# Reordering the prologue, the column sums and the kept outputs of a chunked linear-attention and MLP kernel

## The chip, the cores and the metric

The kernel runs on one core of a Trainium2 chip. A core has five engines that run their own instruction queues in order and meet at semaphores: TensorE (PE in the profile; its weight loads are listed as PEld), VectorE (DVE), ScalarE (ACT), GpSimd (POOL) and SyncE (SP). DMAs are issued here by SP's queue (SPq) and, for a few, by ScalarE's (ACTq). The metric is device time in microseconds of one execution. The kernel before takes 203.81 us, the median of three runs (203.07 to 204.19).

## The reference

Inputs are q, k, v and alpha, each (4 batches, 8 heads, 768 positions, 48), and the weights w_in (384 x 2048), w_out (2048 x 384) and two scalars s and b, all float32.

```python
# per batch and head, for t = 0..767
state = alpha[t][:, None] * state + outer(k[t], v[t])
y[t]  = q[t] @ state
# then, with x = y of all heads side by side, (3072, 384)
h   = x @ w_in
g   = s * relu(h)**2 + b
out = g @ w_out
```

## The kernel before

**Blocks.** The 3072 rows are 24 blocks of 128 positions, six per batch. Within a block the recurrence is written as matrix products; from block to block of a batch a state is carried. All of a block's work is cut into steps, each a small function that issues instructions on one or more engines. `n` or `g` is the block, `u` a quarter.

- `ln(n)` (ScalarE, L200): logarithm of alpha. `cum(n)`: running sums by a matmul with a triangular matrix (L207), then ScalarE's two exponentials `bi_sb` (L218) and `b_sb` (L219). For block 0 to 4 the block's decay comes from further small matmuls; for later blocks `decay(n)` takes it through DRAM by three small DMAs on SP (L227, L229).
- `qk(n)` (VectorE): `kb = k * bi` (L235) and `qb = q * b` (L236). `vcast(n)` (GpSimd, L203): v to bf16.
- `tr(n)`: eight transposes on TensorE (L241), and VectorE's copy of them, `qkT` (L246). `amat(n)`: eight matmuls (L256) that give the scores, and VectorE's two multiplications with the mask, `am_a` and `am_b` (L264).
- `yp(n)`: the block's y from the carried state (L275) and the masked scores (L284), the state's update (L295), and ScalarE's copy of y to bf16 (L302). `st(n)`: the state (VectorE L329 or L331, GpSimd L336 and L340). `xt(n)`: three transposes of y (L309) and ScalarE's copy (L315).
- `mp`, `rl`, `sq` of a block and quarter: 12 matmuls with w_in (L362), ScalarE's relu (L376), VectorE's square (L383). `mr` is the first two, `m` all three.
- `o(n, u)`: 4 matmuls with w_out (L397) that accumulate in one PSUM bank over the four quarters; the last evicts. For the first `NKEEP = 5` blocks ScalarE copies the result into a buffer of its own, `keep_sb` (L406), and VectorE adds the bias later, `add_bias` (L417). For all others VectorE adds the bias while it evicts (L410). Then SP stores (L414).

The scalar s is folded into w_out when it is cast to bf16. The scalar b becomes a row that is added to every output row: b times the column sums of w_out. `colsum(1..7)` (VectorE, L172 and L174, 128 x 768 float32 each) add up eight parts of w_out, `bias_sum` (L177) halves the result once more, and `bias_row` (three times two float32 matmuls L181, and ScalarE's L182) sums over partitions.

**Weights.** w_in comes in four quarters and w_out in four, by DMA in float32. `win(i)` casts a quarter of w_in: one third by ScalarE (L151), two thirds by VectorE (L153). `wout(i)` casts a quarter of w_out: the even ones by ScalarE (L165), the odd ones by VectorE (L157).

**Order.** The order on every engine is written by hand. Each step is put into a list with a position, and the list is sorted by it. A block has 8 positions: block n's `yp` and `st` are at 8n, and its other steps at fixed distances before and after. In the later blocks `cum` is 14.8, `tr` 10.8 and `amat` 7.9 positions ahead of `yp`; for blocks 5 to 7 the distances grow from 7.0, 4.8 and 2.2 to these. The start, with blocks 0 to 3 and the preparation of block 4, is an explicit list (positions 0 to about 10). Where TensorE would have nothing to do there, `busy(n)` issues n matmuls whose result nobody reads (L190).

**Loads.** SP issues the loads of blocks 0 and 1, w_in, w_out and the blocks up to 7, in an order of their own; there are 8 buffers per input. `early(2)` issues alpha and k of block 2 from ScalarE's queue.

Of the kernel before, what the change touches and what calls it, by code (L numbers as in the profile page):

```python
# [8 lines left out]
FP32 = mybir.dt.float32  # L9
BF16 = mybir.dt.bfloat16  # L10
AF = mybir.ActivationFunctionType
# [3 lines left out]
def kernel(  # L15
# [12 lines left out]
    nc = tc.nc  # L28
# [6 lines left out]
    d_model = moe_w_in.shape[0]  # L35
    d_ff = moe_w_in.shape[1]
    NJ = d_ff // 128
    KT = d_model // 128
# [4 lines left out]
    NLD = 8  # L43
# [19 lines left out]
    def ring(name, shape, dtype, n):  # L63
        return [sb.tile(shape, dtype, name=f"{name}{i}") for i in range(n)]
# [25 lines left out]
    t1_sb = sb.tile([128, NP, 96], FP32, name="t1_sb")  # L90
    sc_sb = sb.tile([128, NP, 96], FP32, name="sc_sb")
    sd_sb = ring("sd_sb", [128, NP, 96], BF16, 2)
    r_sb = ring("r_sb", [128, 512], BF16, 6)
    out_sb = ring("out_sb", [128, d_model], FP32, 3)
    xd_all = sb.tile([128, UNITS, KT * C], BF16, name="xd_all")
    gt_all = sb.tile([128, UNITS, NJ * C], BF16, name="gt_all")
# [7 lines left out]
    w_in_st = sb.tile([128, KT, d_ff], FP32, name="w_in_st")  # L104
    w_in_bf = sb.tile([128, KT, d_ff], BF16, name="w_in_bf")
# [2 lines left out]
    cs_sb = sb.tile([128, 2, d_model], FP32, name="cs_sb")  # L108
    bias_w = sb.tile([128, d_model], FP32, name="bias_w")

    NKEEP = 5
    keep_sb = ring("keep_sb", [128, d_model], FP32, NKEEP)


    def src(t, n):
        b, c = n // NCH, n % NCH
        return t[b, :, c * C : (c + 1) * C, :].rearrange("h s d -> s h d")

    def load_a(n, eng=None):
        (eng or nc.sync).dma_start(out=al_sb[n % NLD], in_=src(alpha, n))  # L120

    def load_q(n, eng=None):
        (eng or nc.sync).dma_start(out=q_sb[n % NLD], in_=src(q, n))

    def load_k(n, eng=None):
        (eng or nc.sync).dma_start(out=k_sb[n % NLD], in_=src(k, n))

    def load_v(n, eng=None):
        (eng or nc.sync).dma_start(out=v_sb[n % NLD], in_=src(v, n))

    def load(n):
        if n < NBLK:
            load_a(n)
            load_k(n)
            load_q(n)
            load_v(n)

    def load_w_in(i):
        cols = slice(i * d_ff // 4, (i + 1) * d_ff // 4)
        nc.sync.dma_start(  # L140
            out=w_in_st[:, :, cols], in_=moe_w_in[:, cols].rearrange("(t r) f -> r t f", t=KT)
        )

    def load_w_out(j0, j1):
        nc.sync.dma_start(
            out=w_out_st[:, j0:j1],
            in_=moe_w_out[128 * j0 : 128 * j1, :].rearrange("(j r) m -> r j m", r=128),
        )

    def cast_w_in(c0, c1):  # L150
        nc.scalar.activation(out=w_in_bf[:, 0, c0:c1], in_=w_in_st[:, 0, c0:c1], func=AF.Copy)  # L151
        for kk in (1, 2):
            nc.vector.tensor_copy(out=w_in_bf[:, kk, c0:c1], in_=w_in_st[:, kk, c0:c1])  # L153

    def cast_w_out(j0, j1):
        if j0 // 4 % 2 == 1:
            nc.vector.tensor_scalar(  # L157
                out=w_out_bf[:, j0:j1],
                in0=w_out_st[:, j0:j1],
                scalar1=s_col,  # L160
                scalar2=None,
                op0=ALU.mult,
            )
        else:
            nc.scalar.activation(  # L165
                out=w_out_bf[:, j0:j1], in_=w_out_st[:, j0:j1], func=AF.Copy, scale=s_col
            )
# [177 lines left out]
    nrelu = [0]  # L345


    h_in_o = {(2, 2), (2, 3)}
    h_of = {}

    def mp(g, u):
# [39 lines left out]
    def mm2(g, t, u):  # L391
# [12 lines left out]
        if u == 3:  # L404
            if g < NKEEP:
                nc.scalar.activation(out=keep_sb[g], in_=op[:, 0:d_model], func=AF.Copy)  # L406
# [18 lines left out]
    quarter = d_ff // 4  # L425
# [3 lines left out]
    load_v(2)  # L429
    load_w_in(2)  # L430
    load_w_in(3)
    load(3)
    for j in range(0, NJ, 4):
        load_w_out(j, j + 4)
    for n in range(4, NLD):
        load(n)
    make_upper_triangular(nc, U_bf, 1.0, diag=True)
    for t in la_sb:
# [14 lines left out]
    def at(pos, fn, *args):  # L453
        events.append((pos, len(events), fn, args))
# [3 lines left out]
        st(n)  # L458

    def wout(i):  # L460
        cast_w_out(4 * i, 4 * i + 4)

    def early(n):
        load_a(n, nc.scalar)
        load_k(n, nc.scalar)

    def win(i):
        cast_w_in(i * quarter, (i + 1) * quarter)

    def m(g, u):  # L470
        mp(g, u)
# [11 lines left out]
    for pos, what in enumerate(  # L483
        [
            (ln, 0), (vcast, 0), (cum, 0), (qk, 0), (spread,), (busy, 3), (tr, 0), (busy, 1), (ln, 1), (vcast, 1), (amat, 0),
            (cum, 1), (early, 2), (busy, 3), (yp, 0), (qk, 1), (st, 0), (busy, 1), (tr, 1), (xt, 0), (busy, 2), (amat, 1),
            (win, 0), (win, 1), (busy, 5), (yp, 1), (mr, 0, 0), (st, 1), (busy, 1), (xt, 1), (mr, 0, 1), (ln, 2), (sq, 0, 0),
            (sq, 0, 1), (m, 1, 0), (cum, 2), (mr, 1, 1), (vcast, 2), (qk, 2), (sq, 1, 1), (busy, 4), (tr, 2), (busy, 3),
            (amat, 2), (busy, 5), (yp, 2), (win, 2), (st, 2), (busy, 2), (xt, 2), (m, 2, 0), (m, 2, 1), (ln, 3), (mr, 0, 2),
            (mr, 1, 2), (cum, 3), (vcast, 3), (win, 3), (sq, 0, 2), (sq, 1, 2), (qk, 3), (m, 2, 2), (mr, 0, 3), (mr, 1, 3),  # L490
            (tr, 3), (sq, 0, 3), (sq, 1, 3), (mr, 2, 3), (amat, 3), (sq, 2, 3), (wout, 0), (busy, 4), (yp, 3), (st, 3),
            (wout, 1), (o, 0, 0), (xt, 3), (o, 1, 0), (o, 2, 0), (m, 3, 0), (m, 3, 1), (wout, 2), (o, 0, 1), (o, 1, 1),
            (colsum, 1), (m, 3, 2), (ln, 4), (m, 3, 3), (wout, 3), (o, 2, 1), (cum, 4), (o, 0, 2), (vcast, 4), (qk, 4),
            (o, 1, 2), (o, 2, 2), (colsum, 2), (tr, 4), (o, 1, 3), (colsum, 3), (o, 2, 3), (amat, 4), (colsum, 4), (o, 0, 3),
        ]
    ):
        at(0.1 * pos, *what)


    for i, pos in ((5, 35.6), (6, 39.4), (7, 43.4)):  # L500
        at(pos, colsum, i)
    at(47.4, bias_sum)
    for i in range(3):
        at(51.2 + i, bias_row, i)
    for n in range(NKEEP):
        at(61.3 + 8 * n, add_bias, n)
        at(62.2 + 8 * n, store, n, keep_sb[n])
    for u in range(4):
        at((30.5, 31.5, 33.5, 36.5)[u], o, 3, u)
    at(20.0, load, NLD)  # L510
    for n in range(4, NBLK):
        p = 8 * n
        if n > 4:
            f = min((n - 5) / 3.0, 1.0)
            c, t, a = 7.0 + 7.8 * f, 4.8 + 6.0 * f, 2.2 + 5.7 * f
            at(p - c - 1.9, ln, n)
            at(p - c + 0.01, vcast, n)
            at(p - c, cum, n)
            at(p - c + 0.2, qk, n)
            at(p - t, tr, n)  # L520
            at(p - a, amat, n)
        at(p, y, n)
        if n + 5 < NBLK:
            at(p - 4.0, load, n + NLD - 3)
        for u in range(4):
            at(p + (2.5, 3.5, 5.5, 7.5)[u], m, n, u)
            at(p + (8.5, 9.5, 12.5, 14.5)[u], o, n, u)
        at(p + 1.0, xt, n)
# [32 lines left out]
```

## Time and profile before

| | |
|---|---|
| median of 3 runs | 203.81 us |
| the profiled execution | 203.28 us, of which the instructions span 201.4 us |
| TensorE busy | 184.3 us (92%), 2430 matmuls |
| VectorE busy | 153.6 us (76%) |
| ScalarE busy | 116.8 us (58%) |
| GpSimd busy | 58.6 us (29%) |
| granted TensorE clock | 1.0 throughout |
| DMA | 30.33 MB, mean 151 GB/s; 106611 of 113310 packets under 512 B |
| the 34 fill matmuls (L190) | 10.2 us of TensorE's busy time |
| chain that ended last | TensorE 71%, ScalarE 4%, VectorE 3% |

A row of a timeline gives the start, the duration, engine, line, operation, the tile written and those read, the shape and the count; in brackets stands how long the engine was idle just before, and what ended that. Matmuls are pipelined: one of 128 columns lasts 0.22 us in its row, but they follow each other every 0.056 us, so a chain of them is read by its length and not by its sum. The chain view follows the end of the run back, at each step to what released it.

### The profile page before, as it was taken

What the parts mean: (1) busy time and instruction counts of PE and PEld (TensorE: products, weight loads), DVE (VectorE), ACT (ScalarE), POOL (GpSimd) and SP (SyncE); (2) the same over time, 40 slices, a digit from 0 to 9 for tenths busy, and PEclk for the clock granted to TensorE, in tenths of its full rate; (3) what the DMA queues carried; (4) which work ended last, traced back from release to release, by engine and by line L of the source; (5) the groups of instructions that cost most, each with busy time, mean ns of one, the idle gap of its engine ahead of it and who ended that gap; (6) DMA issues with size and microseconds to landing.
All of it is one profiled execution on the core that took longest, in us unless ns stands there. A gap on an engine that the chain in (4) does not pass through costs nothing.

```text
span 201.4 us, 6040 instructions
## 1 busy us (share of the span) xinstructions
PE 184.3 (92%) x2430; PEld 142.5 (71%) x2430; DVE 153.6 (76%) x293; ACT 116.8 (58%) x236; POOL 58.6 (29%) x96
## 2 busy tenths in 40 slices
PE   1987987997789799999999999999999999999993
PEld 1546576773576587878788787778888877877781
DVE  4586757578587888999997889988976998896431
ACT  3347277582565566657566665756666675654540
POOL 5154040410320052354140235414500651451000
PEclk9999999999999999999999999999999999999999
DMA  7999989999999485693995695695879482111102
GB/s 127 191 337 239 276 202 373 256 196 188 166 188 190 58 143 84 136 169 82 246 211 99 146 217 111 109 154 106 184 150 171 86 144 64 21 39 42 39 3 78
DMA packets 113310, 30.33 MB, mean 151 GB/s; under 512 B 106611, under 2 KB 111746, under 8 KB 113282
## 3 DMA queue, kind: packets, MB, share of 16 engines
q1 hardware_dynamic: 111198, 29.55, 74.4%
q10 hardware_dynamic: 2084, 0.39, 1.4%
q8 instruction: 19, 0.31, 0.7%
q14 instruction: 9, 0.07, 0.1%
HBM read 25.19 MB, written 4.74 MB: 149 GB/s over the span
## 4 chain that ended last, share of the span: by engine, by line
PE 71%; ACT 4%; DVE 3%; issue 3%; DVEq 0%; ACTq 0%
PE o_ps L397 26%; PE h_ps L362 26%; PE ct_ps L241 5%; PE a_ps L256 3%; PE a_ps L397 3%; PE y_ps L284 2%; PE h_ps L309 2%; ACT r_sb L376 1%; PE y_ps L275 1%; PE ct_ps L207 1%; PE p_ps L295 1%; DVE qb_sb L236 1%; ACT w_out_bf L165 1%; DVE am_b L264 1%; DVE kb_sb L235 1%
## 5 line engine op out<-in xcount | busy, mean ns | idle before, releaser
L376 ACT ACTIVATE r_sb<-h_ps 128x512 bf16<-128x512 f32 x94 | 56.1, 597 | 44.0 <-PE h_ps L362 42.4
L362 PE MATMUL h_ps<-xd_all,w_in_bf 128*128 128x128 bf16 x1128 | 74.6, 219 | 1.8 <-ACT w_in_bf L151 1.0
L362 PEld LDWEIGHTS <-w_in_bf 128*128 128x128 bf16 x1152 | 69.2, 98 | 8.4 <-ACT w_in_bf L151 1.2
L397 PE MATMUL o_ps<-w_out_bf,gt_all 128*128 128x384 bf16 x336 | 68.3, 326 | 0.6 <-ACT keep_sb L406 0.6
L383 DVE TENSOR_TENSOR gt_all<-r_sb 128x512 bf16<-128x512 bf16 x96 | 45.0, 481 | 30.1 <-ACT r_sb L376 29.5
L336 POOL TENSOR_TENSOR sd_sb<-t_sb,blast 48x192 bf16<-48x192 f32 x40 | 20.8, 520 | 113.2 <-DVE t_sb L331 74.5
L397 PEld LDWEIGHTS <-gt_all 128*128 128x128 bf16 x384 | 33.9, 98 | 17.5 <-issue 0.8
L203 POOL CAST v_bf<-v_sb 128x384 bf16<-128x384 f32 x24 | 17.9, 752 | 11.6 <-DMA v_sb<-in_v_dram 11.4
L236 DVE TENSOR_TENSOR qb_sb<-q_sb,b_sb 128x384 bf16<-128x384 f32 x24 | 20.4, 852 | 0.0
L315 ACT ACTIVATE xd_all<-h_ps 128x384 bf16<-128x384 bf16 x24 | 11.8, 491 | 14.6 <-PE h_ps L309 14.6
L246 DVE COPY qkT<-ct_ps 112x1024 bf16<-112x1024 bf16 x24 | 16.4, 684 | 3.6 <-PE ct_ps L241 3.5
L264 DVE TENSOR_TENSOR am_a<-a_ps,mask 128x512 bf16<-128x512 f32 x24 | 16.4, 683 | 2.2 <-PE a_ps L256 2.2
L340 POOL TENSOR_TENSOR sc_sb<-t_sb,blast 112x384 f32<-112x384 f32 x16 | 17.6, 1100 | 1.3
L235 DVE TENSOR_TENSOR kb_sb<-k_sb,bi_sb 128x384 bf16<-128x384 f32 x24 | 13.7, 571 | 4.8 <-ACT bi_sb L218 4.6
L264 DVE TENSOR_TENSOR am_b<-a_ps,mask 128x512 bf16<-128x512 f32 x24 | 16.3, 681 | 0.0
L302 ACT ACTIVATE y_bf<-y_ps 128x384 bf16<-128x384 f32 x24 | 11.7, 486 | 7.0 <-PE y_ps L284 7.0
L200 ACT ACTIVATE la_sb<-al_sb 128x384 bf16<-128x384 f32 x24 | 12.4, 516 | 3.7 <-DMA al_sb<-in_alpha_dram 3.7
L241 PEld LDWEIGHTS <-qb_sb 128*112 128x112 bf16 x96 | 7.7, 132 | 7.9 <-DVE qb_sb L236 7.4
L218 ACT ACTIVATE bi_sb<-ct_ps 128x384 f32<-128x384 f32 x24 | 11.7, 486 | 2.2 <-PE ct_ps L210 2.0
L241 PE MATMUL ct_ps<-ident,qb_sb 128*112 128x128 bf16 x96 | 10.1, 229 | 2.8 <-DVE qb_sb L236 2.6
L207 PE MATMUL ct_ps<-la_sb,U_bf 128*128 128x384 bf16 x24 | 8.0, 333 | 4.9 <-ACT la_sb L200 4.9
L219 ACT ACTIVATE b_sb<-ct_ps 128x384 f32<-128x384 f32 x24 | 11.9, 494 | 0.0
(64 smaller groups left out, 186.1 us busy)
## 6 DMA issues: line engine op xcount, KB each, us to landing
q_sb<-in_q_dram SPq DMA_DIRECT2D x24, 192.0 KB, 4.6
v_sb<-in_v_dram SPq DMA_DIRECT2D x24, 192.0 KB, 4.3
al_sb<-in_alpha_dram SPq DMA_DIRECT2D x23, 192.0 KB, 3.2
k_sb<-in_k_dram SPq DMA_DIRECT2D x23, 192.0 KB, 3.7
out_dram<-out_sb SPq DMA_DIRECT2D x19, 192.0 KB, 1.9
w_in_st<-in_moe_w_in_dram SPq DMA_DIRECT2D x4, 768.0 KB
w_out_st<-in_moe_w_out_dram SPq DMA_DIRECT2D x4, 768.0 KB
out_dram<-keep_sb SPq DMA_DIRECT2D x5, 192.0 KB
```

The costliest lines, as they stand in the source:

```text
L203: nc.gpsimd.tensor_copy(out=v_bf[n % 3], in_=v_sb[n % NLD])
L235: nc.vector.tensor_tensor(out=kb_sb[n % 3][:, :, 0:48], in0=k_sb[n % NLD], in1=bi_sb[n % 2], op=ALU.mult)
L236: nc.vector.tensor_tensor(out=qb_sb[n % 2][:, :, 0:48], in0=q_sb[n % NLD], in1=b_sb[n % 2], op=ALU.mult)
L241: nc.tensor.transpose(out=t_ps[0:112, x, p, :], in_=t.rearrange("a h d -> a (h d)")[:, 128 * p : 128 * p + 112], identity=ident,)
L246: nc.vector.tensor_copy(out=qkT_sb[n % 2][0:112].rearrange("a x p t -> a (x p t)"), in_=t_ps[0:112].rearrange("a x p t -> a (x p t)"),)
L264: nc.vector.tensor_tensor(out=am_sb[e][n % 2], in0=a_ps[e], in1=mask4, op=ALU.mult)
L336: nc.gpsimd.tensor_tensor(out=sd[r, :, d], in0=t1_sb[r, :, d], in1=bl[r].to_broadcast([48, NP, 48]), op=ALU.mult)
L340: nc.gpsimd.tensor_tensor(out=sc_sb[0:112], in0=t1_sb[0:112], in1=bl[0:112].to_broadcast([112, NP, 96]), op=ALU.mult)
L362: nc.tensor.matmul(out=hp[:, jj * N : (jj + 1) * N], lhsT=w_in_bf[:, kk, 128 * j : 128 * (j + 1)], rhs=xd_sb[g][:, kk, 0:N], start=(kk == ...
L376: nc.scalar.activation(out=rs, in_=h_of.pop((g, u)), func=AF.Relu)
L383: nc.vector.tensor_tensor(out=gt_sb[g][:, u * 512 : (u + 1) * 512], in0=rs, in1=rs, op=ALU.mult)
L397: nc.tensor.matmul(out=op[:, 0:d_model], lhsT=gt_sb[g][:, j * N + t * C : j * N + (t + 1) * C], rhs=w_out_bf[:, j, :], start=(j == 0), sto ...
```

## The change

Six things change together.

1. `win(2)` and `win(3)` move: the third quarter's casts stand behind `tr(2)` and ahead of the masks of block 2, the fourth's ahead of `st(2)`; the fourth is cast by VectorE alone. `mr(0,2)`, `mr(1,2)`, `mr(0,3)`, `mr(1,3)`, and block 2's quarters follow them earlier; four fill matmuls ahead of `yp(2)` go. Other quarters than before use the `o_ps` bank for their first product, and the ring of relu results has 8 buffers, not 6.
2. Of blocks 3 and 4, alpha and k are issued by ScalarE's queue (`early(3)` behind `ln(2)`, `early(4)` behind relu (2,3)); SP issues only their q and v.
3. The first quarter of w_out is cast half by ScalarE, half by VectorE.
4. The order around block 4 changes (`o` ahead of `tr(4)`, `ln(4)` behind `m(3,3)`), and blocks 5 to 7 are started up to two positions earlier.
5. `colsum(3..7)`, `bias_sum` and `bias_row` move from the prologue and the slots up to 6 into slots 8 to 13 (a slot is the 8 positions behind 8n).
6. 13 blocks' outputs are kept instead of 5, in the space where w_in was staged; their adds and stores follow from position 117.3 on, one every 5.5 positions. Before, the five adds were at 61.3 to 93.3.

```diff
-    r_sb = ring("r_sb", [128, 512], BF16, 6)
+    r_sb = ring("r_sb", [128, 512], BF16, 8)
...
-    NKEEP = 5
-    keep_sb = ring("keep_sb", [128, d_model], FP32, NKEEP)
+    NKEEP = 13
+    keep_all = w_in_st.rearrange("a t f -> a (t f)")
+    keep_sb = [keep_all[:, d_model * n : d_model * (n + 1)] for n in range(NKEEP)]
...
-    def cast_w_in(c0, c1):
-        nc.scalar.activation(out=w_in_bf[:, 0, c0:c1], in_=w_in_st[:, 0, c0:c1], func=AF.Copy)
-        for kk in (1, 2):
+    def cast_w_in(c0, c1, act):
+        if act:
+            nc.scalar.activation(out=w_in_bf[:, 0, c0:c1], in_=w_in_st[:, 0, c0:c1], func=AF.Copy)
+        for kk in range(act, KT):
             nc.vector.tensor_copy(out=w_in_bf[:, kk, c0:c1], in_=w_in_st[:, kk, c0:c1])
-    def cast_w_out(j0, j1):
-        if j0 // 4 % 2 == 1:
+    def cast_w_out(j0, j1, act):
+        if not act:
...
-    h_in_o = {(2, 2), (2, 3)}
+    h_in_o = {(1, 3), (2, 2)}
...
-    load(3)
+    load_q(3)
+    load_v(3)
     for j in range(0, NJ, 4):
         load_w_out(j, j + 4)
-    for n in range(4, NLD):
+    load_q(4)
+    load_v(4)
+    for n in range(5, NLD):
         load(n)
...
     def wout(i):
-        cast_w_out(4 * i, 4 * i + 4)
+        if i == 0:
+            cast_w_out(0, 2, True)
+            cast_w_out(2, 4, False)
+        else:
+            cast_w_out(4 * i, 4 * i + 4, i == 2)
...
     def win(i):
-        cast_w_in(i * quarter, (i + 1) * quarter)
+        cast_w_in(i * quarter, (i + 1) * quarter, int(i < 3))
...
-            (win, 0), (win, 1), (busy, 5), (yp, 1), (mr, 0, 0), (st, 1), (busy, 1), (xt, 1), (mr, 0, 1), (ln, 2), (sq, 0, 0),
-            (sq, 0, 1), (m, 1, 0), (cum, 2), (mr, 1, 1), (vcast, 2), (qk, 2), (sq, 1, 1), (busy, 4), (tr, 2), (busy, 3),
-            (amat, 2), (busy, 5), (yp, 2), (win, 2), (st, 2), (busy, 2), (xt, 2), (m, 2, 0), (m, 2, 1), (ln, 3), (mr, 0, 2),
-            (mr, 1, 2), (cum, 3), (vcast, 3), (win, 3), (sq, 0, 2), (sq, 1, 2), (qk, 3), (m, 2, 2), (mr, 0, 3), (mr, 1, 3),
-            (tr, 3), (sq, 0, 3), (sq, 1, 3), (mr, 2, 3), (amat, 3), (sq, 2, 3), (wout, 0), (busy, 4), (yp, 3), (st, 3),
-            (wout, 1), (o, 0, 0), (xt, 3), (o, 1, 0), (o, 2, 0), (m, 3, 0), (m, 3, 1), (wout, 2), (o, 0, 1), (o, 1, 1),
-            (colsum, 1), (m, 3, 2), (ln, 4), (m, 3, 3), (wout, 3), (o, 2, 1), (cum, 4), (o, 0, 2), (vcast, 4), (qk, 4),
-            (o, 1, 2), (o, 2, 2), (colsum, 2), (tr, 4), (o, 1, 3), (colsum, 3), (o, 2, 3), (amat, 4), (colsum, 4), (o, 0, 3),
+            (win, 0), (win, 1), (busy, 5), (yp, 1), (mr, 0, 0), (st, 1), (busy, 1), (xt, 1), (ln, 2), (early, 3), (mr, 0, 1),
+            (sq, 0, 0), (sq, 0, 1), (m, 1, 0), (cum, 2), (mr, 1, 1), (vcast, 2), (qk, 2), (sq, 1, 1), (busy, 4), (tr, 2),
+            (win, 2), (busy, 3), (amat, 2), (busy, 1), (mr, 0, 2), (mr, 1, 2), (yp, 2), (win, 3), (st, 2), (sq, 0, 2),
+            (sq, 1, 2), (busy, 2), (ln, 3), (xt, 2), (mr, 0, 3), (cum, 3), (mr, 1, 3), (vcast, 3), (qk, 3), (mr, 2, 0),
+            (sq, 0, 3), (mr, 2, 1), (mr, 2, 2), (tr, 3), (sq, 1, 3), (mr, 2, 3), (early, 4), (amat, 3), (sq, 2, 0), (wout, 0),
+            (busy, 4), (yp, 3), (sq, 2, 1), (st, 3), (o, 0, 0), (sq, 2, 2), (sq, 2, 3), (wout, 1), (xt, 3), (o, 1, 0),
+            (o, 2, 0), (m, 3, 0), (m, 3, 1), (wout, 2), (o, 0, 1), (o, 1, 1), (colsum, 1), (m, 3, 2), (m, 3, 3), (ln, 4),
+            (wout, 3), (o, 2, 1), (cum, 4), (o, 0, 2), (vcast, 4), (qk, 4), (o, 1, 2), (o, 2, 2), (colsum, 2), (o, 0, 3),
+            (o, 1, 3), (o, 2, 3), (tr, 4), (o, 3, 0), (amat, 4),
...
-    for i, pos in ((5, 35.6), (6, 39.4), (7, 43.4)):
-        at(pos, colsum, i)
-    at(47.4, bias_sum)
+    for i in range(3, 8):
+        at(69.3 + 8 * (i - 3), colsum, i)
+    at(109.3, bias_sum)
     for i in range(3):
-        at(51.2 + i, bias_row, i)
+        at(109.6 + i, bias_row, i)
     for n in range(NKEEP):
-        at(61.3 + 8 * n, add_bias, n)
-        at(62.2 + 8 * n, store, n, keep_sb[n])
-    for u in range(4):
-        at((30.5, 31.5, 33.5, 36.5)[u], o, 3, u)
+        at(117.3 + 5.5 * n, add_bias, n)
+        at(118.2 + 5.5 * n, store, n, keep_sb[n])
+    for u in range(1, 4):
+        at((30.5, 31.2, 32.5)[u - 1], o, 3, u)
...
-            c, t, a = 7.0 + 7.8 * f, 4.8 + 6.0 * f, 2.2 + 5.7 * f
+            c, t, a = 9.0 + 5.8 * f, 5.8 + 5.0 * f, 3.4 + 4.5 * f
```

## The prediction

> **What bounds the kernel now.** I read the busy table, then the chain of waits in order of time, the stage table, and the timelines of TensorE, VectorE and the DMA queues.
>
> ```profile
> span 201.4 us, 6040 instructions
> PE 184.3 (92%) x2430; PEld 142.5 (71%) x2430; DVE 153.6 (76%) x293; ACT 116.8 (58%) x236; POOL 58.6 (29%) x96
> ```
> ```profile
> 80.01 1.34 PE h_ps L362 x24
> ...
> 82.50 0.67 PE h_ps L362 x12
> 83.17 0.65 PE o_ps L397 x4
> ...
> 87.10 1.34 PE h_ps L362 x24
> ```
>
> In the chain, everything from about 70 us on is TensorE: a quarter of the first product (12 matmuls) takes 0.67, a quarter of the second (4) 0.65, and a whole block repeats after 87.10 - 80.01 = 7.09. So from there the end moves only if TensorE starts that stage earlier or stalls in it. Before 70 us the chain hops between TensorE, ScalarE and VectorE:
>
> ```profile
> 52.00:77.00 25.00, 21.60 (x293) 16.77 (x291) 19.63 (x35) 15.60 (x34) 5.81 (x9) 1.00 0.95 142
> 80.00:110.00 30.00, 30.00 (x426) 24.39 (x423) 27.43 (x51) 19.25 (x40) 10.49 (x15) 1.00 0.80 158
> 120.00:170.00 50.00, 50.00 (x704) 40.43 (x705) 42.27 (x78) 31.59 (x65) 17.45 (x24) 1.00 0.70 132
> ```
>
> Columns: stretch, its length, then busy time of TensorE, its weight loads, VectorE, ScalarE, GpSimd, granted clock (full throughout), DMA. TensorE is idle for 3.4 of the 25 us, and not at all from 80 to 110 or 120 to 170. VectorE has 42.27 / 50 x 7.09 = 5.99 us of work per block late in the run: 1.1 us of room per block, and that is what the second half of the change draws on. The stalls themselves, on TensorE:
>
> ```profile
> 31.71 1.51 PE L362 MATMUL h_ps<-xd_all,w_in_bf 128*128 128x128 bf16 x24 [1.02 <-ACT w_in_bf L151]
> ...
> 55.58 0.43 PE L241 MATMUL ct_ps<-ident,qb_sb 128*112 128x128 bf16 x4 [0.91 <-DVE qb_sb L236]
> ...
> 60.09 0.20 PE L284 MATMUL y_ps<-v_bf,am_a 128*128 128x48 bf16 x1 [0.39 <-DVE am_a L264]
> ...
> 68.21 0.43 PE L241 MATMUL ct_ps<-ident,qb_sb 128*112 128x128 bf16 x4 [1.25 <-DVE qb_sb L236]
> ```
>
> and the VectorE work ahead of them in its order (column sums), with a late block for comparison:
>
> ```profile
> 57.97 0.95 DVE L174 TENSOR_TENSOR cs_sb<-cs_sb,w_out_st 128x768 f32<-128x768 f32 x1
> ...
> 64.74 0.95 DVE L174 TENSOR_TENSOR cs_sb<-cs_sb,w_out_st 128x768 f32<-128x768 f32 x1
> ...
> 175.45 0.55 DVE L410 TENSOR_TENSOR out_sb<-o_ps,bias_w 128x384 f32<-128x384 f32 x1
> 176.43 0.42 DVE L383 TENSOR_TENSOR gt_all<-r_sb 128x512 bf16<-128x512 bf16 x1 [0.43 <-ACT r_sb L376]
> ...
> 178.93 1.18 DVE L236 TENSOR_TENSOR qb_sb<-q_sb,b_sb 128x384 bf16<-128x384 f32 x1
> ```
> ```profile
> 9.68 0.42 ACTq L120 DMA_DIRECT2D al_sb<-in_alpha_dram  x1
> 10.14 0.89 ACTq L126 DMA_DIRECT2D k_sb<-in_k_dram  x1
> 17.16 4.32 SPq L126 DMA_DIRECT2D k_sb<-in_k_dram  x1
> ```
>
> **The change part by part.** I place each part by the first matmul of y(n), the block's attention output: before, y(3) at 35.9, y(4) 51.7, y(5) 59.4, y(6) 69.4, y(7) 77.2.
>
> *Up to y(3): gain 1.7.* Issuing a and k of block 3 costs ScalarE's queue 0.42 + 0.89 = 1.3 us at about 18 us, ahead of relu(0,1) and the two exponentials of block 2; 0.85 of that lies in ScalarE's gaps, so the transposes of block 2 go from 21.5 to about 21.95. The copy of their result (0.69) ends at 23.3. The third quarter's casts then come on VectorE ahead of the masks (two, 0.75): 24.1. m(0,2) and m(1,2) fill 1.35 us of TensorE where four fill matmuls (0.41 each in the rows, issued every 0.21) went: 25.5. y(2) (0.54) waits for them and ends at 26.1, against 24.95; ScalarE, after two relus of 0.6, copies it by 26.7. The last quarter's casts are all VectorE's now (three, 1.1), ahead of state(2), whose only user is y(3): hidden. ln(3) could run at 26.7. Its alpha was issued at about 18.4, and block 2's, issued the same way, took 7.9 us to land beside w_in: 26.3 at best, 28 if its packets wait for all of w_in; I take 27.5. From there ln, the transposed-output copy and a relu (0.5 to 0.6 each) lead to 29.1, two exponentials (0.49) and relu(1,3) to 30.7, m(2,2) (0.67) to 31.4, and the transposes of block 3 follow, at 33.07 before: 1.7 gained. Ends: 2.4 with alpha in time; 0.4 if k3 takes on ScalarE's queue what the row of SP's issue shows beyond its own (4.32 - 0.89 = 3.4), of which gaps hide 2.1. The row at 10.14 was taken while SP's queue was stuck too (an issue of 2.65 at 9.63), so I stay near the short price.
>
> [...]
>
> *y(3) to y(4): gain 1.1.* w_out's first quarter is halved: ScalarE 0.8 instead of 1.57, VectorE half of 1.01. The VectorE half stands behind masks and sq(2,0), so o(0,0) waits some 0.4. ln(4) behind relu(3,3) makes cum(4) wait 0.5. Against that, seven o-quarters instead of three stand between cum(4) and the transposes, which covers the exponentials and products of block 4 (stall 0.46 before), and o(0,3) ahead of o(1,3) and o(2,3) hides its eviction (0.7). Two column sums (1.9) leave VectorE's order. y(4) comes at 49.7 instead of 51.7, with o(3,2) (0.65) and cum(5) (0.16) already done: 2.0 - 1.7 + 0.8 = 1.1.
>
> *y(4) to y(7): gain 2.9 net.* Three column sums (0.95) and the bias sum (0.55) leave, and blocks 5 to 7 start one to two positions sooner. y(4) to y(5), before 7.6: TensorE has 5.0 us of work (four quarters at 0.67, o(3,3) 0.65, y 0.54, transposes 0.62, scores and cum 0.5), VectorE 5.4, and a wait for the masks of some 0.75 stays: 5.9. y(5) to y(6), before 10.0: 7.0 of work, 0.45 stall, some 0.4 of small ones: 7.85. y(6) to y(7), before 7.85: 7.1. So y(7) comes at 70.6 instead of 77.2; 6.6 less the 0.9 of bias matmuls that only move later gives 5.7 for the three parts (1.7 + 1.1 + 2.9).
>
> *Loads.* Decay rows stand behind the load of block 10 on SP (first at 64.7, landing near 70.5). state(6) would want them at 65, but y(7) uses the result at 70.6: hidden by 2 us of cover; without it, 1 to 2.
>
> *Blocks 5 to 12: cost 0.5.* ScalarE's copy (0.49) takes the place of VectorE's add (0.55). It stands between relu 2 and relu 3 and delays relu 3, and with it the chain sq, masks, products, transposes, which has no room (178.93 + 1.18 = 180.11; the transposes start at 180.16), by about 0.15 where GpSimd's state work runs beside it. Bounds 0 (VectorE's freed 0.55 pays) to 8 x 0.3 = 2.4. The five column sums (0.95) replace two adds (1.09) there: nothing.
>
> *Slot 13: cost 1.0.* The bias sum now stands 0.3 positions ahead of the first bias matmul, not 3.8. In the late block the transposes start at 173.06, m's third quarter ends its issue at 174.22, and the copy that stands ahead of the sum ends at 174.59; with 0.55 the sum is done at 175.15: TensorE waits 175.2 - 174.2 = 1.0, with o, m and y behind it. Bounds 0.6 to 1.4.
>
> *Slots 14 to 22: cost 0.6.* Thirteen adds, 1.45 per block x 0.54 = 0.79: VectorE 6.78 of 7.09. Ten fall after the products, where the waits of 0.53 and 0.43 in the late block absorb them. Three (positions 128.3, 144.8, 161.3) stand ahead of them and delay the transposes by 0 to 0.55 each; as the second product shrinks from 1.18 to 0.55 where GpSimd has finished, I take 0.2. Bounds 0 to 5.2 (first rival).
>
> SP's thirteen stores wait for these adds, and loads and decay rows queue behind; both are due over 10 positions later.
>
> Sum: 5.7 - 0.5 - 1.0 - 0.6 = 3.6. The profiled execution took 203.28 (span 201.4 and 1.9 around it), 0.53 below the median of 203.81; 203.81 - 3.6 = 200.2.
>
> **The rivals.** *VectorE becomes the bound in slots 14 to 22.* If adds of two SBUF tensors are stretched beside GpSimd as qb is (1.18), a block needs 5.99 + 1.45 x 1.18 = 7.70, 0.61 over 7.09, for 8.5 blocks: 5.2 instead of 0.6. Then 203.81 - (5.7 - 1.5 - 5.2) = 204.8: slower. It decides once the adds mean over 0.76 us (1.1 / 1.45), and ends above 203.81 over 1.1. For it: qb. Against: five keep adds before meant 0.544.
>
> *Block 3's and 4's inputs come late, or their issue holds ScalarE.* The gain to y(3) is 0.4 instead of 1.7, and the same 1.3 is lost once more where block 4's issues stand ahead of w_out's cast and the copy of y(3): 5.7 - 2 x 1.3 = 3.1, less 2.1: 202.8, the edge of no change. For it: SP's issues of 3.6 to 4.3 in this stretch; against: ScalarE's own of 0.42 and 0.89.
>
> *The stalls have another cause than the column sums.* If qb's exponentials on ScalarE set them, y(4) to y(7) gains 1.0: 3.8 - 2.1 = 1.7, 202.1.
>
> **How the numbers follow.** Forecast 0.58, own range 197.5 to 202.4 (early 4.5 to 7.3, late 1.0 to 3.1). VectorE rival 0.18, late inputs 0.14, other cause 0.10. Half a per cent, 1.0 us, is about what a measurement of this kernel can tell from no change: faster below 202.8, slower above 204.8. Faster: 0.56 of the forecast, 0.07 of the other cause, 0.04 of late inputs: 0.67. Slower: 0.14 of the VectorE rival (its lower end is no change) and 0.04 of late inputs with ScalarE held longer: 0.18. Same: the remaining 0.15. The range runs from 197.5 to 204.9, which takes in most of each.
>
> **What would show it.** Right: y(4) near 49.7 and y(7) near 70.6; no column sum from the fourth on before 70 us; no wait of 1.25 for qb before y(6); a wait of about 1.0 at the first bias matmul in slot 13; adds near 0.55; period 7.09 after slot 14. Wrong: ACTq issues over 2 us near 18 or 32; ln(3) waiting for alpha past 28; TensorE waiting for qb or the masks in slots 14 to 22, or adds over 0.76.

## The result and the profile after

The changed kernel takes 203.12 us, the median of 22 runs (201.21 to 204.07), against 203.80 for the kernel before, measured beside it: a ratio of 0.9953, 95% interval 0.993 to 0.9976. That is a gain of some 0.7 to 1.0 us where 3.6 were forecast. The profiled execution took 204.07, with a span of 202.2; it is the slowest of the 22.

The busy line of its page, in the order of the first fence of the prediction (line numbers here and below are those of the kernel that ran):

```profile
span 202.2 us, 6091 instructions
PE 186.5 (92%) x2426; PEld 144.6 (72%) x2426; DVE 151.3 (75%) x295; ACT 118.8 (59%) x243; POOL 63.7 (31%) x96
```

TensorE has four matmuls fewer than before (2426, not 2430), and is busy 2.2 us longer. That speaks for a slower clock, and the stage table shows where (stretch, length, busy time of PE, PEld, DVE, ACT and POOL with counts, granted clock, DMA share, GB/s):

```profile
35.00:52.00 17.00, 14.08 (x118) 9.22 (x115) 9.03 (x16) 8.85 (x16) 3.90 (x5) 0.90 1.21 200
52.00:77.00 25.00, 23.91 (x337) 18.50 (x337) 18.35 (x37) 16.23 (x34) 4.76 (x8) 1.00 0.85 136
120.00:170.00 50.00, 48.23 (x680) 39.30 (x679) 42.12 (x81) 31.02 (x64) 18.48 (x23) 1.00 0.65 131
```

From 52 to 77 TensorE does 337 matmuls instead of 293, as hoped. From 35 to 52, which the prediction did not show, it does 118 at a clock of 0.90. From 120 on it is idle for 1.8 us, where before it was never idle.

I lay both executions side by side by the first matmul of y(n). The row of forecast is the prediction's sum, spread over the same stretches. The last column is the second experiment, which differs from the changed kernel in one step's place and is told of below.

| stretch (us) | before | forecast | after | block 4's a and k sooner |
|---|---|---|---|---|
| start to y(0) | 10.1 | 10.1 | 11.1 | 11.3 |
| y(0) to y(3) | 25.7 | 24.0 | 22.8 | 22.9 |
| y(3) to y(4) | 15.8 | 15.5 | 20.1 | 16.0 |
| y(4) to y(7) | 25.5 | 20.9 | 21.15 | 21.15 |
| y(7) to y(13) | 42.1 | 42.6 | 41.9 | 42.0 |
| y(13) to y(14) | 7.1 | 9.0 | 9.8 | 9.8 |
| y(14) to y(22) | 56.3 | 56.9 | 56.5 | 56.5 |
| y(22) to the end | 18.8 | 18.8 | 18.8 | 18.8 |
| span | 201.4 | 197.8 | 202.2 | 198.4 |

One stretch is out by 4.6 us, y(3) to y(4). One is out by 0.8, y(13) to y(14). The chain of waits, followed back from 40 us, names the first (start, duration, what):

```profile
27.32 8.78 DMA w_out_st<-in_moe_w_out_dram
36.09 0.02 issue
36.11 0.38 ACTq L128
36.49 0.05 issue
36.54 0.94 ACT w_out_bf L168
37.48 0.04 issue
37.52 1.28 PE o_ps L400 x4
```

Read it upwards. TensorE's first o (L400) waits for ScalarE's half of the cast of w_out's first quarter (L168). The cast does not wait for data of its own: it stands in ScalarE's queue behind the issue of block 4's k (L128). That issue waits for a transfer of w_out, the third of its four quarters, issued at 27.32. The timelines of ScalarE and of VectorE add the rest:

```profile
32.69 0.37 ACTq L122 DMA_DIRECT2D al_sb<-in_alpha_dram  x1
36.11 0.38 ACTq L128 DMA_DIRECT2D k_sb<-in_k_dram  x1
36.54 0.93 ACT L168 ACTIVATE w_out_bf<-w_out_st,sb_col 128x768 bf16<-128x768 f32 x1 [3.27 <-DMA w_out_st<-in_moe_w_out_dram]
```
```profile
34.73 0.61 DVE L160 TENSOR_SCALAR w_out_bf<-w_out_st,sb_col 128x768 bf16<-128x768 f32 x1
```

Alpha's issue at 32.69 is over in 0.37 us. ScalarE ends the relu that it has in hand at 33.27 (36.54 less the idle of 3.27), and then stands still until 36.11. The row of the cast blames a DMA of w_out_st, which reads as if the quarter that it casts had not landed. But VectorE cast the other half of that same quarter at 34.73, so it had. In the trace the DMAs share eight semaphores in turn (101 to 105 and 107 to 109), and the issue of this k waits for 101, which had been used before by the third quarter of w_out, issued at 27.32. The third quarter is cast only later.

The idle has an aftermath. Stage table, the 3.4 us after the idle and the 3.4 us after that:

```profile
37.71:41.13 3.42, 3.42 (x14) 1.72 (x13) 0.28 (x1) 0.63 (x2) 1.47 (x2) 0.50 1.46 192
41.13:44.54 3.41, 3.41 (x45) 2.81 (x44) 1.49 (x3) 2.29 (x3) 0.50 (x1) 1.00 0.97 165
```

TensorE is busy throughout, at half the clock: 3.41 us of half speed are 1.7 us lost. Together with the idle of 2.47 ahead of them that makes up the 4.1 us by which this stretch exceeds the 16.0 of the second experiment.

The second place, in slot 13, has the two waits of TensorE:

```profile
123.80 0.49 PE L184 MATMUL y_ps<-cs_sb,ones_f 128*128 128x128 f32 x2 [0.82 <-DVE cs_sb L180]
126.94 0.34 PE L278 MATMUL y_ps<-sd_sb,qkT 112*128 112x96 bf16 x4 [0.83 <-ACT bias_w L185]
```

The first is the wait for the bias sum that was forecast at 1.0. The second was not forecast. The third bias row puts its product into the `y_ps` bank, and stands directly ahead of y(14), which wants that bank: y(14) waits until ScalarE has copied the row out.

Late in the run nothing happened. The 13 adds (duration in ns: least, median, most) and, from the same run, a product `qb` that is stretched to 1.18 beside GpSimd as before (0.55 at 151.61, with GpSimd idle), which the first rival feared for the adds:

```profile
L420 DVE TENSOR_TENSOR w_in_st<-w_in_st,bias_w x13: 545/548/554, 132.9 to 190.3; 128x384 f32<-128x384 f32 x13
```
```profile
179.70 1.18 DVE L239 TENSOR_TENSOR qb_sb<-q_sb,b_sb 128x384 bf16<-128x384 f32 x1
```

### The profile page after: what moved, and what is told of

The parts are those of the page before. It is cut to its first block, busy times and chain, and to the rows that moved or that the text cites. A ratio compares the mean times of both kernels' runs of the same rounds, so it can differ in the third digit from the quotient of the medians.

```text
span 202.2 us, 6091 instructions
## 1 busy us (share of the span) xinstructions
PE 186.5 (92%) x2426; PEld 144.6 (72%) x2426; DVE 151.3 (75%) x295; ACT 118.8 (59%) x243; POOL 63.7 (31%) x96
## 3 DMA queue, kind: packets, MB, share of 16 engines
q10 hardware_dynamic: 6244, 1.18, 4.2%
## 4 chain that ended last, share of the span: by engine, by line
PE 75%; DMA 10%; SPq 4%; ACT 4%; DVE 3%; issue 1%; ACTq 0%; DVEq 0%
PE o_ps L400 27%; PE h_ps L365 26%; DMA al_sb<-in_alpha_dram 5%; PE ct_ps L244 5%; DMA w_out_st<-in_moe_w_out_dram 4%; PE a_ps L400 4%; PE a_ps L259 3%; SPq L147 2%; PE ct_ps L210 2%; SPq L131 2%; PE h_ps L312 2%; PE y_ps L287 2%; ACT r_sb L379 2%; PE y_ps L278 1%; PE p_ps L298 1%
## 5 line engine op out<-in xcount | busy, mean ns | idle before, releaser
L400 PE MATMUL o_ps<-w_out_bf,gt_all 128*128 128x384 bf16 x336 | 69.0, 328 | 2.6 <-ACT w_out_bf L168 2.5
L339 POOL TENSOR_TENSOR sd_sb<-t_sb,blast 48x192 bf16<-48x192 f32 x40 | 21.5, 538 | 106.2 <-DVE t_sb L334 64.0
L400 PEld LDWEIGHTS <-gt_all 128*128 128x128 bf16 x384 | 34.5, 99 | 20.1 <-issue 3.8
L206 POOL CAST v_bf<-v_sb 128x384 bf16<-128x384 f32 x24 | 18.6, 782 | 14.3 <-DMA v_sb<-in_v_dram 14.1
L343 POOL TENSOR_TENSOR sc_sb<-t_sb,blast 112x384 f32<-112x384 f32 x16 | 21.4, 1335 | 1.3
L318 ACT ACTIVATE xd_all<-h_ps 128x384 bf16<-128x384 bf16 x24 | 11.8, 490 | 15.8 <-PE h_ps L312 15.8
L238 DVE TENSOR_TENSOR kb_sb<-k_sb,bi_sb 128x384 bf16<-128x384 f32 x24 | 14.2, 593 | 4.8 <-ACT bi_sb L221 4.7
L239 DVE TENSOR_TENSOR qb_sb<-q_sb,b_sb 128x384 bf16<-128x384 f32 x24 | 16.7, 695 | 0.0
L244 PEld LDWEIGHTS <-qb_sb 128*112 128x112 bf16 x96 | 8.5, 136 | 5.0 <-DVE qb_sb L239 3.6
L244 PE MATMUL ct_ps<-ident,qb_sb 128*112 128x128 bf16 x96 | 10.2, 231 | 0.5 <-DVE qb_sb L239 0.5
```

What stands on the lines that cost most here:

```text
L206: nc.gpsimd.tensor_copy(out=v_bf[n % 3], in_=v_sb[n % NLD])
L238: nc.vector.tensor_tensor(out=kb_sb[n % 3][:, :, 0:48], in0=k_sb[n % NLD], in1=bi_sb[n % 2], op=ALU.mult)
L239: nc.vector.tensor_tensor(out=qb_sb[n % 2][:, :, 0:48], in0=q_sb[n % NLD], in1=b_sb[n % 2], op=ALU.mult)
L244: nc.tensor.transpose(out=t_ps[0:112, x, p, :], in_=t.rearrange("a h d -> a (h d)")[:, 128 * p : 128 * p + 112], identity=ident,)
L339: nc.gpsimd.tensor_tensor(out=sd[r, :, d], in0=t1_sb[r, :, d], in1=bl[r].to_broadcast([48, NP, 48]), op=ALU.mult)
L343: nc.gpsimd.tensor_tensor(out=sc_sb[0:112], in0=t1_sb[0:112], in1=bl[0:112].to_broadcast([112, NP, 96]), op=ALU.mult)
```

## The experiments

All ratios are to the kernel before, measured on the same chip in the same set, with 95% intervals.

### Block 4's alpha and k issued by SP

```diff
-    load_q(4)
-    load_v(4)
-    for n in range(5, NLD):
+    for n in range(4, NLD):
...
-            ... (mr, 2, 3), (early, 4), (amat, 3), (sq, 2, 0), (wout, 0),
+            ... (mr, 2, 3), (amat, 3), (sq, 2, 0), (wout, 0),
```

> The changed kernel with alpha and k of block 4 issued by SP again (load(4) whole), so that ScalarE's queue issues nothing behind relu(2,3). Theory A (ScalarE's queue was held from 32.7 to 36.1 us by the issue of block 4's k, which waits until an earlier DMA has landed, and w_out's cast stood behind it): the cast on ScalarE starts by 34.2, o(0,0) waits under 0.5 us instead of 2.5, the clock stays full, y(4) starts at 50 instead of 54.1, the time is 203.1 - 2.1 - 1.6 = 199.4. Theory B (w_out's first quarter itself lands at 36.5, as the waits view names it): the cast starts at 36.5 as before, y(4) at 54, time 203.

Measured: 200.48 us, ratio 0.9804 (0.9767 to 0.9842). y(3) to y(4) is 16.0 (33.8 to 49.7), and the clock stays full. So 4.1 of the 4.6 us by which this stretch was out came with the two issues. That y(4) comes at 49.7, the very time forecast, is partly luck: y(3) came 0.4 sooner than forecast, and the stretch is 0.5 longer. The time is 1.1 above what was written down; 0.7 of that is lost at y(6) to y(7) (7.8 instead of 7.1), for a reason that the run on block 3's loads shows below.

### The same two issues, but sooner

```diff
-            (sq, 1, 2), (busy, 2), (ln, 3), (xt, 2), ...
+            (sq, 1, 2), (busy, 2), (ln, 3), (early, 4), (xt, 2), ...
-            ... (mr, 2, 3), (early, 4), (amat, 3), ...
+            ... (mr, 2, 3), (amat, 3), ...
```

> The changed kernel with block 4's alpha and k still issued by ScalarE's queue, but right behind ln(3) instead of behind relu(2,3). Theory A: the issue now has to wait only for q of block 3, which has landed by then; no hold, or under 1 us near 28 us; y(4) near 50, time 199.4 to 200. Theory B: same as the changed kernel, 203, or later, since w_out's packets share the DMA engines with block 4's for longer. A third reading, that issuing on ScalarE's queue is what costs, whatever it waits for: x1 gains and x2 does not.

Measured: 200.34 us, ratio 0.9805 (0.9763 to 0.9847). ScalarE's timeline there:

```profile
27.44 0.37 ACTq L122 DMA_DIRECT2D al_sb<-in_alpha_dram  x1
27.85 0.60 ACTq L128 DMA_DIRECT2D k_sb<-in_k_dram  x1
33.37 0.93 ACT L168 ACTIVATE w_out_bf<-w_out_st,sb_col 128x768 bf16<-128x768 f32 x1
```

Now k's issue takes 0.60 and the cast runs at 33.37, 3.2 us sooner than in the changed kernel. The issue itself is cheap on ScalarE's queue. What cost was its place, some 5 us later, where the semaphore that it shares belonged to a large transfer still under way. So it is not the issuing queue that costs, and the change's idea was sound: one step stood in the wrong place.

### Fill matmuls in the idle

```diff
-            (busy, 4), (yp, 3), (sq, 2, 1), ...
+            (busy, 4), (yp, 3), (busy, 12), (sq, 2, 1), ...
```

> The changed kernel with 12 more fill matmuls (nobody reads their result) between y(3) and o(0,0), where TensorE waits 2.5 us. 12 x 0.215 = 2.6 us lie in the wait. If the idle time there is what halves the granted clock for 3.4 us afterwards (37.7 to 41.1 in the profile of the changed kernel), the clock stays at 1.0, the slow matmuls of that stretch win back about 1.6 us, and all runs lie near 201.5. If the clock has another cause: 203.1, and the half clock is still there.

Measured: 202.32 us, ratio 0.9886 (0.9849 to 0.9923), 0.8 above what was written down. The idle is still there, filled with work that nobody reads, and y(3) to y(4) is 18.4 instead of 20.1. All six executions had a mean clock of at least 0.997. So the 4.1 us split into about 2.4 of waiting (18.4 against 16.0) and 1.7 of clock.

### A shorter fill, and the changed kernel once more

```diff
-            (busy, 4), (yp, 3), (sq, 2, 1), ...
+            (busy, 4), (yp, 3), (busy, 4), (sq, 2, 1), ...
```

> The changed kernel with 4 fill matmuls (about 0.85 us) behind y(3) instead of the 12 of the third run, so that the idle before the first o goes from 2.5 to about 1.6 us while ScalarE's queue is held as before. Theory A (the length of the idle decides whether the clock is halved; an idle of 1.6 left it full in one profile): no execution shows a mean clock of 0.992 or less, and all lie near 201.4, the lower group of the changed kernel. [...]

Measured: 201.73 us, ratio 0.9889 (0.9861 to 0.9917), six executions from 201.57 to 202.16, all with a clock of at least 0.997. The times lie some 0.3 above what was written down. The idle was 1.21 us behind the fills in the profiled execution. This agrees with theory A: with the shorter idle the clock was not halved once in six executions. What the length of an idle has to do with it is taken up at the end.

> The changed kernel itself once more, for a second profile. If the clock explains its two groups of times: each execution with a mean clock of 0.997 or more lies at 201.2 to 201.8, each with 0.989 to 0.992 at 202.9 to 204.1, and nothing between. If something else makes the groups (the loads, for one), a time in the upper group comes with a full clock.

Measured: 202.48 us, the median of 12 (201.74 to 204.02), ratio 0.9929 (0.9896 to 0.9961). Seven executions had a clock of at least 0.998 and took 201.74 to 202.51; five had 0.989 to 0.992 and took 203.43 to 204.02. The lower group is wider than was written down (four of the seven lie at 202.15 to 202.51), but none of the upper group had a full clock, and the groups still part by their clock. The first 22 executions split in the same way: seven at 201.21 to 201.75 with a clock of at least 0.997, fifteen at 202.93 to 204.07 with 0.989 to 0.992. The profile of this set is of the lower group. There k's issue came free at 35.38 instead of 36.11, TensorE's idle was 1.67 us, and no clock was lost:

```profile
35.38 0.37 ACTq L128 DMA_DIRECT2D k_sb<-in_k_dram  x1
36.79 0.81 PE L400 MATMUL o_ps<-w_out_bf,gt_all 128*128 128x384 bf16 x4 [1.67 <-ACT w_out_bf L168]
```

So the change's time has two values, which part by the clock. That the moment at which the DMA lands decides between them is not shown: these are two profiles, and they also differ in when the clock first went full (13.8 and 9.0 us).

### The bias sum and its rows further apart

```diff
-    at(109.3, bias_sum)
+    at(105.65, bias_sum)
     for i in range(3):
-        at(109.6 + i, bias_row, i)
+        at((107.55, 109.55, 109.6)[i], bias_row, i)
```

> The changed kernel with the bias sum at position 105.65 instead of 109.3 and the bias rows at 107.55, 109.55 and 109.6 instead of 109.6, 110.6 and 111.6. If the waits at 123.8 (bias sum, 0.8 to 1.0) and 126.9 (y(14) behind ScalarE's copy of the last bias row, 0.8 to 1.05) are what slot 13 costs, both go, the distance y(13) to y(14) falls from 9.8 to about 7.9 us, and the time is 203.1 - 1.9 = 201.2. If VectorE has no room in that slot, the waits come back at the transposes of block 15 or at the masks, and the gain is under 1.

Measured: 199.99 us, ratio 0.9804 (0.9757 to 0.9852). y(13) to y(14) falls from 9.8 to 8.4. The wait of y(14) is gone and that for the sum is smaller:

```profile
118.95 0.49 PE L184 MATMUL y_ps<-cs_sb,ones_f 128*128 128x128 f32 x2 [0.38 <-DVE cs_sb L180]
```

Both causes of slot 13 are thereby shown. Only 1.4 of the 3.1 us to the changed kernel is theirs: four of the six executions had a full clock, and in the profiled one the idle ahead of the first o was 1.64, as in the lower group above.

### Only the late part, only the early part

Late part alone: the kernel before with the column sums, bias and kept outputs of the change.

```diff
-    NKEEP = 5
+    NKEEP = 13
...
-    for i, pos in ((5, 35.6), (6, 39.4), (7, 43.4)):
-        at(pos, colsum, i)
-    at(47.4, bias_sum)
+    for i in range(3, 8):
+        at(69.3 + 8 * (i - 3), colsum, i)
+    at(109.3, bias_sum)
```

(with the bias rows, adds and stores of the change, and `colsum` 3 and 4 taken out of the explicit list).

> The kernel before with only the late part of the change: column sums 3 to 7 in slots 8 to 12, bias sum and rows in slot 13, 13 kept outputs. Theory of the prediction: y(4) to y(7) falls from 25.5 to about 22.5, slot 13 costs 2.0 (waits) and 0.9 of bias matmuls moves there: 203.8 - 3.0 + 2.0 = 202.8. Rival: y(4) to y(7) stays near 24.5, and the time is 204.8.

Measured: 205.46 us, ratio 1.0068 (1.0048 to 1.0089): slower by 0.7%. y(4) to y(7) is 24.2, against 25.5 before, and 0.8 of that is the six bias matmuls that left (y(6) to y(7), where they stood, falls from 7.86 to 7.09, the period of a block). So taking the column sums off VectorE brought 0.5 us there. TensorE's timeline has the same two waits for `qb` as before, the first unchanged (0.90, against 0.91), the second smaller (0.71, against 1.25):

```profile
56.40 0.43 PE L242 MATMUL ct_ps<-ident,qb_sb 128*112 128x128 bf16 x4 [0.90 <-DVE qb_sb L237]
...
68.50 0.43 PE L242 MATMUL ct_ps<-ident,qb_sb 128*112 128x128 bf16 x4 [0.71 <-DVE qb_sb L237]
```

And VectorE's own timelines tell why the first did not shrink: VectorE was itself idle ahead of it, for ScalarE's exponentials, and by as much in the kernel before (the first of the two) as here.

```profile
54.13 0.62 DVE L235 TENSOR_TENSOR kb_sb<-k_sb,bi_sb 128x384 bf16<-128x384 f32 x1 [1.03 <-ACT bi_sb L218]
```
```profile
54.96 0.62 DVE L236 TENSOR_TENSOR kb_sb<-k_sb,bi_sb 128x384 bf16<-128x384 f32 x1 [1.03 <-ACT bi_sb L219]
```

Early part alone: the second experiment, with the column sums, the bias and 5 kept outputs as in the kernel before.

```diff
-    NKEEP = 13
+    NKEEP = 5
...
-    for i in range(3, 8):
-        at(69.3 + 8 * (i - 3), colsum, i)
-    at(109.3, bias_sum)
+    for i, pos in ((5, 35.6), (6, 39.4), (7, 43.4)):
+        at(pos, colsum, i)
+    at(47.4, bias_sum)
```

(with the bias rows, adds and stores of the kernel before, and `colsum` 3 and 4 back in the explicit list).

> x2 with the column sums, the bias sum, the bias rows and the kept outputs where they are in the kernel before (5 kept outputs, column sums 3 and 4 around the preparation of block 4): the early part of the change alone. Theory of the prediction (column sums in VectorE's order set the stalls of y(4) to y(7)): that distance rises from 21.2 us (x2) to about 24.5, slot 13 gives 2.0 back, bias matmuls 0.9 in either: 200.4 + 2.4 - 2.0 = 200.8 or more. Rival (the earlier start of blocks 5 to 7 took the stalls away): the distance stays at 22 and the time falls to 199.

Measured: 199.13 us, ratio 0.9763 (0.974 to 0.9787). That is 1.2 us better than the second experiment, which has the late part too. y(4) to y(7) is 23.1, of which 0.8 are bias matmuls, so 22.3; with the column sums gone it is 21.15. Here they cost 1.2. So from y(4) on the late part wins 1.96 up to y(7) (1.19 by the column sums, 0.77 by the bias matmuls) and 0.17 up to y(13), and loses 2.74 in slot 13 and 0.22 behind it: 0.8 in all. The spans of the two profiles differ by 1.1; the intervals of the two ratios overlap.

### Blocks 5 to 7 started as late as before

```diff
-            c, t, a = 9.0 + 5.8 * f, 5.8 + 5.0 * f, 3.4 + 4.5 * f
+            c, t, a = 7.0 + 7.8 * f, 4.8 + 6.0 * f, 2.2 + 5.7 * f
```

(in the second experiment; column sums, bias and kept outputs stay those of the change.)

> Block 4's a and k sooner, as in the second run, but blocks 5 to 7 are started as late as in the kernel before (the formula of the distances is the old one); column sums, bias and keep copies are those of the changed kernel. Theory (the sooner start of blocks 5 to 7 is what took away most of the stalls between y(4) and y(7), about 2.4 us): y(4) to y(7) goes from 21.2 back to 23 to 24, with TensorE waiting for qb, kb or the masks ahead of y(5) to y(7), and the time is 202 to 203. Rival (the order of the o steps, and the column sums gone from VectorE, took them away): y(4) to y(7) stays within 0.5 of 21.2 and the time at 200.3.

Measured: 203.35 us, ratio 0.9987 (0.997 to 1.0003), 3.0 above the second experiment. y(4) to y(7) is 24.3 instead of 21.15, and the waits are back with no column sum near them:

```profile
54.41 0.43 PE L244 MATMUL ct_ps<-ident,qb_sb 128*112 128x128 bf16 x4 [1.26 <-DVE qb_sb L239]
...
66.02 0.43 PE L244 MATMUL ct_ps<-ident,qb_sb 128*112 128x128 bf16 x4 [0.71 <-DVE qb_sb L239]
```

With the two runs above, and the bias matmuls taken out, y(4) to y(7) makes a square:

| y(4) to y(7), us, without the bias matmuls | column sums in the prologue | column sums later |
|---|---|---|
| blocks 5 to 7 started as before | 24.7 (before) | 24.2 and 24.3 |
| started sooner | 22.3 | 21.15 |

The lead is worth 2.4 to 3.1, the column sums 0.5 to 1.2. The two values in the upper right cell also say that the rest of the early part, the order of the o steps among it, does next to nothing in this stretch: the run with 24.2 has the old order, the one with 24.3 the new.

### Block 3's alpha and k on SP too

```diff
-    load_q(3)
-    load_v(3)
+    load(3)
...
-            ... (ln, 2), (early, 3), (mr, 0, 1),
+            ... (ln, 2), (mr, 0, 1),
```

(on top of the first experiment.)

> x1 with block 3's alpha and k issued by SP too, ahead of q and v, so that ScalarE's queue issues nothing but block 2's: the part of the change that moves block 3's loads, undone. By the reading that a second issuing queue saves only issue time: no later arrival of alpha, ScalarE's relu(0,1) 0.5 sooner, y(3) at 33.3 to 33.9 as in x1 (33.8), time 200.0 to 200.5. By the prediction's reading (alpha for block 3 comes sooner by ScalarE's queue): ln(3) waits for alpha to 28.5 or more, y(3) at 35, time 201.5.

Measured: 201.23 us, ratio 0.9861 (0.9831 to 0.9891), 0.75 above the first experiment, with intervals that overlap; the stretches tell more. y(0) to y(3) is 22.6, against 22.5: the issuing queue did nothing for block 3. ln(3) even ran at 25.99 without a wait for alpha, where it ran at 27.10 after a wait of 0.29 in the first experiment. The loss stands elsewhere, at y(6) to y(7): 8.4, against 7.8 with two issues on SP and 7.1 with none. ScalarE's timeline of this run shows how:

```profile
68.33 0.49 ACT L222 ACTIVATE b_sb<-ct_ps 128x384 f32<-128x384 f32 x1 [2.35 <-DMA row_dr<-b_sb]
```

The exponential `b_sb` of a later block reuses a buffer that the decay row's DMA still reads. That DMA stands in SP's queue behind the loads, so each further issue on SP makes it later: its issue is at 63.52 in the changed kernel, 64.87 with two more on SP and 65.44 with four. qb and the transposes then wait behind ScalarE (1.15 on TensorE in this run).

### Both places mended

```diff
-    at(109.3, bias_sum)
+    at(105.65, bias_sum)
     for i in range(3):
-        at(109.6 + i, bias_row, i)
+        at((108.55, 109.55, 109.6)[i], bias_row, i)
```

(on top of the second experiment.)

> The changed kernel with both found waits taken out: block 4's alpha and k issued right behind ln(3) (as in x2), and the bias sum at 105.65 with the bias rows at 108.55, 109.55 and 109.6. If the two waits are separate and each is lost for good on TensorE: 200.4 (x2) - 1.5 (what x4 showed in slot 13) - 0.5 (the wait of the first bias row, which x4 still had) = 198.4; y(4) at 50, y(13) to y(14) 7.95. If they overlap in effect, over 199.5.

Measured: 198.88 us, ratio 0.9741 (0.9715 to 0.9767). y(13) to y(14) is 8.7; what is left there is a wait of 0.67 of the first row for the sum.

```diff
-    at(105.65, bias_sum)
+    at(103.3, bias_sum)
     for i in range(3):
-        at((108.55, 109.55, 109.6)[i], bias_row, i)
+        at((107.55, 108.55, 109.55)[i], bias_row, i)
```

> Block 4's a and k sooner, as in the second run, and the bias sum now in slot 12 (position 103.3), its three rows one position apart from each other (107.55, 108.55, 109.55). Theory (what is left at slot 13 with the sum at 105.65 is that the sum still ends after the first row wants it, 0.7 to 0.8 us): the wait of the first row for the sum goes, y(13) to y(14) is 7.05 + 0.9 for the row matmuls = 7.95 instead of 8.7, and the time falls from 198.9 to 198.1. Rival (VectorE has no room in slot 12 either, so the sum only delays the masks or products of the next block there): y(12) to y(13) or y(13) to y(14) grows by 0.5 or more elsewhere and the time stays at 198.9.

Measured: 198.51 us, ratio 0.9732 (0.9718 to 0.9746). y(13) to y(14) is 7.8, the forecast 7.95 or a little better, and the stage table has TensorE busy throughout from 97 us, ahead of y(11), to 120, the last bias row:

```profile
97.00:120.00 23.00, 23.00 (x324) 19.07 (x320) 19.87 (x36) 15.78 (x34) 7.43 (x10) 1.00 0.72 123
```

The step in time is 0.4, not 0.8, and the intervals of the two overlap. Still this is the fastest of all, 5.3 us under the kernel before and 4.6 under the change as made; against the early part alone (199.13) the late part now seems to pay, by 0.6, though the intervals still overlap a little.

## Why the prediction was wrong, and where it was right

**Up to y(3): right in size, partly by another way.** Forecast 1.7, measured 1.9 in the profiled execution (35.9 to 34.0); in the other profiles with this order of the start y(3) comes at 33.3 to 34.7. ln(3) ran at 27.56, where 27.5 was taken for alpha. But the price of the two issues mattered little: with block 3 wholly on SP the distance y(0) to y(3) is the same within 0.1. The gain is there without the moved issues too, so it came from the rest of the change in this stretch, which is mainly the order of the casts and quarters; these were not tested apart. What ScalarE's queue does save is time on SP's queue, and it shows 45 us later, at the decay rows.

**y(3) to y(4): this step failed.** The sum gave block 4's two issues no term here at all. Measured, they cost 4.1 us in the profiled execution, the slowest of the 22: 2.4 of waiting and 1.7 of clock. By the medians of the changed kernel and the second experiment they cost 2.8 (203.12 to 200.34), and in the profile of the lower group 1.65 (17.62 against 15.97), all of it waiting. Two things went wrong. First, the issues were priced by the durations of their rows (0.42 and 0.89), and the hold stands in no issue's row: the row of k's issue is 0.38 long, and the wait lies ahead of it. For the same reason the sign that was written down, a row of over 2 us on ScalarE's queue, did not appear. The long rows of SP's issues, 3.6 to 4.3 us, are no such holds either: the view of what SP's issues waited for is empty in the kernel before from 8 to 52 us, and what made those rows long stays open. The thing to ask was which earlier transfer the issue of block 4's k would find on its semaphore. The second rival named the place exactly, "block 4's issues stand ahead of w_out's cast and the copy of y(3)", and the hold it took, 3.4, is close to what was measured (from 33.06, alpha's issue done, to 36.11: 3.05), but by luck, since it came from those rows of SP. It then subtracted 2.1 of gaps taken from another stretch and so came to 1.3, and gave the case a chance of 0.14. Behind ScalarE stood the first o, which TensorE needs at once; there was no gap to hide in. Second, no case had a clock in it, since the clock was full throughout in the profile of before. Without these two issues in that place the step is nearly right: the stretch is 16.0 in the first experiment, 0.5 over the sum.

**y(4) to y(7): right in size, wrong in cause.** Forecast 20.9, measured 21.15, with y(4) to y(5) 5.8 (forecast 5.9), y(5) to y(6) 8.26 (7.85) and y(6) to y(7) 7.1 (7.1). The prediction named the column sums and the sooner start of the blocks together, and showed the column sums as what stood ahead of the stalls; they are worth 0.5 to 1.2 and the sooner start 2.4 to 3.1. The third rival was right that the stalls had another cause, ScalarE's exponentials, but it took for granted that nothing else in the change would mend it.

**Decay rows.** "Hidden by 2 us of cover" held in the changed kernel (7.1). The cover was smaller than said, and it was not state(6) that used it up first but ScalarE, by the buffer that the row's DMA reads.

**Blocks 5 to 12.** Forecast a cost of 0.5, measured a gain of 0.2 (42.1 to 41.9): ScalarE's copies delayed nothing that TensorE waited for.

**Slot 13.** The wait for the sum was forecast at 1.0 and measured at 0.82. The wait of y(14) for the bank, 0.83, was missed: the text looked at who feeds the bias matmuls and not at who else writes their bank. The bias matmuls themselves, put at 0.9, take 0.7 to 0.8 (7.81 against 7.10 where nothing waits).

**Slots 14 to 22.** Forecast 0.6, measured 0.2, with adds of 0.548. The first rival needed 0.76 and is false: the stretch of qb beside GpSimd, 1.18, was not seen in these adds, of which three (at 144.09, 158.16 and 172.17, 0.55 each) had a row of GpSimd beside them.

## What to carry to other kernels

Before a DMA issue is moved to a compute engine's queue, ask which earlier transfer its semaphore belongs to at that place, and what stands behind it on that engine: here the issue took 0.37 to 0.60 us where it did not have to wait, and was held for 3.05 where it did. That wait did not show as a long issue row, which was 0.38 long. It showed as idle time of 3.27 us ahead of the next compute instruction, put down to a DMA; whether that instruction's own data had landed can be seen from another engine that used them. When a stall ends with one engine, look whether that engine was idle itself just ahead; if it was, removing its other work may bring little, and starting the chain sooner more: here 0.5 to 1.2 and 2.4 to 3.1 us.

## What the runs showed of the hardware

**The clock.** In the profile of the changed kernel an idle of 2.47 us on TensorE was followed by 3.41 us at half clock; idles of 1.64 and 1.67 in two other profiles, and of 1.21 behind fills, were not. Whether the length of the idle alone decides is open, and that an idle of 1.7 is safe is not shown. The times even speak against the length alone, by an estimate: among the first 22 executions the upper group's median is 1.7 us above the lower's (203.27 and 201.56), which is the price of the clock alone (half of 3.41) and leaves nothing for a longer idle.

The hold raises the odds of a lost clock, but it is not the only way to one. A mean clock of 0.992 or less stands in 22 of 40 executions with ScalarE's hold (the changed kernel and the run with the bias rows apart) and in none of 12 where fills shorten the idle. Without the hold it stands in 1 of 6 of the second experiment, 3 of 12 of the run with blocks 5 to 7 as late as before, 3 of the 56 of the kernel before that ran beside the experiments, and none of the 33 of the other runs. Which idle it followed there no profile shows.

**The start.** The first full clock came at 8.4 to 15.1 us in different executions of nearly the same first instructions (8.4 in the profile of the kernel before, 13.8 in that of the changed kernel, where the fill matmuls followed each other every 0.42 us ahead of it and every 0.21 behind it), and y(0) between 10.1 and 11.4: about 10.2 in the profiles where the clock was full by 9 us, 11.1 or later in those where it took 13.7 or more. Much of that is given back by y(3) (34.3 and 34.2 in two runs whose y(0) came at 10.2 and 11.3). Absolute times of two profiles are therefore not to be subtracted in the first 15 us, and y(3) itself still spreads by over 1 us between profiles.
